# Argmax in its PSUM tile, logits turned ahead of the weighted sums, masks on other engines, late weights converted in the first batch

## The chip, the core and the metric

The kernel runs on one core of one Trainium2 chip. The metric is the device time in microseconds (us) of one execution, as a median over several. Four compute engines work side by side, each with a queue of its own that it runs in order: TensorE (PE; PEld is its loading of weights), VectorE (DVE), ScalarE (ACT) and GpSimd (POOL). SyncE (SP) issues nearly all transfers, also in order.

## The reference

The inputs q, k and v have 4 batches, 8 heads, 768 positions and 64 columns per head. In the first part each position attends only to positions of its own cluster; in the second the result x (768 x 512 per batch) is rotated by an angle, mixed over the positions, and passed through a channel product.

```python
q_assign = np.argmax(np.einsum('bhsd,hcd->bhsc', q_n, c_n), axis=-1)   # 16 clusters per head
k_assign = np.argmax(np.einsum('bhsd,hcd->bhsc', k_n, c_n), axis=-1)
mask = q_assign[:, :, :, None] == k_assign[:, :, None, :]
scores = np.where(mask, 0.125 * np.matmul(q, k.transpose(0, 1, 3, 2)), -1e9)
attn = np.exp(scores - np.max(scores, axis=-1, keepdims=True))
attn = attn / (np.sum(attn, axis=-1, keepdims=True) + 1e-09)
x = np.matmul(attn, v)                       # heads side by side: 4 x 768 x 512

theta = x @ w_theta
zr, zi = x * np.cos(theta), x * np.sin(theta)
y = np.einsum('ts,bsd->btd', w_tok_r, zr) + np.einsum('ts,bsd->btd', w_tok_i, zi)
u = x + y
out = u + np.maximum(u @ w_ch, 0.0)
```

q, k, v and the centroids are 32-bit floats. The four weight matrices are 64-bit floats; the kernel loads their raw words and makes 32-bit floats of them itself.

## The kernel before, in words

**Attention.** Two heads make a pair; there are 16 pairs (4 batches of 4). A pair is cut into 12 units (`NU`): 2 halves of the queries (a) times 6 blocks of 128 keys (i). The main loop takes two units per round, u and u + 1. In a round TensorE makes the scores of unit u, then the scores of unit u + 1 interleaved with products that give the row maximum of a unit ten units ahead (`ahead = u + LEAD`). Those products go to tiles "m" of the PSUM pool `ps0`, which has two of them in rotation. `max_of` on the vector engine reduces each to nm (L396). Between the two interleaved halves, j = 1 first and j = 0 second, stand the weighted sums av (L509) of the two units before.

Products are kept exact by splitting a number into a rounded part (hi) and the rest (lo): hq, lq, hk, lk for the pair, hi and lo for each weight. The mask is a product too: mq and mk (128 x 768) hold, at row c of each head, whether a position belongs to cluster c, scaled so that a pair of positions of different clusters gets a huge negative score. Row 32 carries the row maximum to be subtracted.

**Small steps of a pair** are generators whose pieces are filed under unit numbers (`at_unit`, `stages`). A round runs three batches of pieces: those up to u - 0.5 before the weighted sums, those up to u behind them, those up to u + 1 at the end of the round; within a batch in order of the number. `in_order` then chains the instructions of each engine in exactly this order, so in the attention no planner moves them. A planner with its own costs does place the instructions of the second part, and it may begin them while the attention still runs.

`assign(pi)` prepares pair pi two pairs ahead. Its pieces, with the numbers of `A_UNITS` counted from the start of pair pi - 2: load q and k (-9); multiply with the centroids (lg, L263) and copy (-4); turn the logits with three transposes on TensorE into the tile lt (L275), reduce to the maximum (L278) and mark where the logits equal it (eq, L280) (-2); multiply eq by a column of numbers that fall with c (L284) and reduce again, which gives the cluster number with ties to the first (L286) (-1); turn it (2), store it (2), load it back spread over 16 rows per head as clq and clk (3); make mq by an absolute value (L335, 6) and a cut-off at zero (L337, 7) on ScalarE, for pair 1 with one GpSimd instruction (L333); make mk on the vector engine (L339, 7.9). lt takes an "m" tile from pair 2 on. `A_SECOND` and `A_THIRD` are the numbers for pairs 1 and 2.

Other small steps on the same queues: `add_exps` sums the exponentials in threes on GpSimd (L448); `add_sums` adds two such sums on the vector engine (L452) at units 8 and 13 of the pair; `sums` reduces them over the keys, and its row goes through memory in four steps with numbers `SUMS`: store sd, load sq, take the reciprocal (L494) and store, load rb; `normalise` multiplies.

**Weights.** `early_weights` converts w_theta and the first three row blocks (t = 0, 1, 2) of both mixing matrices during the attention: load 768 KB of raw words (L130), an absolute value on ScalarE (L135), four operations on the vector engine (L137, L140, L143, L146), hi on ScalarE (L158), lo on GpSimd (L159). The row blocks t = 3, 4, 5 are converted there too, but kept in DRAM as 32-bit floats (L156, tiles wd3r to wd5i); one block starts every `W_EVERY` = 12 units, sixteen in all.

**Second part.** For each of 24 blocks (b, t) of 128 positions `theta` makes the angle (tp, L608, then kk and r on the vector engine, L613 to L615) and `rotate` the parts z; `mix` multiplies with the row block t of the weights into y (L876), and after t = 5 `channel(b)` makes the channel product (L899). In batch 0, `late` is advanced once per block before its `mix`: it loads a kept block, splits it (L790 on ScalarE, L791 on the vector engine), and from t = 5 on converts w_ch in four row blocks. Its buffers are the four tiles "u" (`u_tile`), which the channel stage then uses for itself. `first_rotation` begins the first block at the end of the attention.

## Time and profile before

| | us |
|---|---|
| median of 3 runs | 791.12 (791.0 to 792.93) |
| profiled execution | 792.87 |
| its span, first to last instruction | 791.1 |
| TensorE busy in the span | 774.3 (98%) |
| VectorE busy | 572.6 (72%) |
| GpSimd busy | 488.3 (62%) |
| ScalarE busy | 386.5 (49%) |
| mean granted TensorE clock | 0.991 of full speed |

The attention fills the span to about 452 us, the second part the rest. In 40 slices of the span (about 20 us each) the busy share, in tenths, reads so; the third row is GpSimd:

```
PE   6999999999999999999999799999999999999998
DVE  5789999999999999999989659954445433634322
POOL 3388789999999999888988432561215122332131
```

In the profile's rows, `out<-in` names the tile written and the tiles read, `[0.58 <-PE m L374]` behind a row says how long the engine sat idle before it and what ended that, and xN is a number of like instructions. TensorE's matmuls overlap, so the busy time of a group can be more than its share of the span.

### The profile page before, as it was taken

To read this page: it belongs to the slowest core of one execution; us is meant where nothing else is said; L and a number is where in the kernel's file an instruction comes from. 1 tells how busy PE (TensorE), PEld (TensorE's weight loads), DVE (VectorE), ACT (ScalarE), POOL (GpSimd) and SP (SyncE) were. 2 spreads that over 40 slices of the span, in tenths; PEclk is the share of its full clock that TensorE was granted. 3 is DMA by queue.
4 is the path that set the end of the run, shared out by engine and by line. 5 is a ranking of instruction groups with operands and counts; after the bars stand their busy time and mean duration, and the time that the engine had idled before them with its cause. 6 is when DMAs were issued, how large, how long until landed. Compare 5 with 4: busy or idle time off the path is not lost.

```text
span 791.1 us, 14306 instructions
## 1 busy us (share of the span) xinstructions
PE 774.3 (98%) x5538; PEld 572.9 (72%) x5538; DVE 572.6 (72%) x688; ACT 386.5 (49%) x777; POOL 488.3 (62%) x284
## 2 busy tenths in 40 slices
PE   6999999999999999999999799999999999999998
PEld 4656665666656565656665488899889988899998
DVE  5789999999999999999989659954445433634322
ACT  3366666767676676767556436341334123403310
POOL 3388789999999999888988432561215122332131
PEclk9899999999999999999999999999999999999999
DMA  3132324332433244324343467115011411030001
GB/s 120 61 98 72 93 95 151 93 123 91 151 104 125 81 149 151 119 84 164 112 161 109 101 182 206 24 31 173 15 27 28 160 27 27 14 94 15 1 21 61
DMA packets 81583, 73.43 MB, mean 93 GB/s; under 512 B 59588, under 2 KB 65324, under 8 KB 81132
## 3 DMA queue, kind: packets, MB, share of 16 engines
q1 hardware_dynamic: 81228, 72.10, 30.5%
q8 instruction: 43, 0.70, 0.4%
q10 hardware_dynamic: 288, 0.43, 0.1%
q14 instruction: 24, 0.20, 0.1%
HBM read 57.08 MB, written 15.32 MB: 92 GB/s over the span
## 4 chain that ended last, share of the span: by engine, by line
PE 91%; DVE 5%; DMA 2%; issue 1%; SPq 1%; ACT 1%; DVEq 0%
PE y L876 26%; PE sc L374 24%; PE av L509 15%; PE tp L608 8%; PE cy L899 5%; PE m L374 4%; PE cp L899 3%; PE sm L476 2%; PE lg L263 2%; PE y L899 1%; DVE acc L452 1%; PE lt L275 1%; DVE nm L396 1%; PE mt L404 1%; DVE xl L583 1%
## 5 line engine op out<-in xcount | busy, mean ns | idle before, releaser
L437 ACT ACTIVATE at<-sc 128x384 f32<-128x384 f32 x384 | 173.6, 493 | 96.0 <-PE m L374 50.5
L396 DVE TENSOR_REDUCE nm<-m 128x1 f32<-128x768 f32 x192 | 179.6, 945 | 21.4 <-PE m L374 18.3
L448 POOL TENSOR_TENSOR acc<-at,at 128x768 f32<-128x768 f32 x64 | 129.9, 2030 | 36.0 <-ACT at L437 36.0
L374 PE MATMUL m<-hk,hq 64*128 64x384 f32 x384 | 147.1, 387 | 0.9 <-DVE nm L396 0.8
L509 PE MATMUL av<-at,vt 128*64 128x384 f32 x768 | 145.7, 499 | 1.4 <-ACT at L437 1.2
L830 POOL TENSOR_TENSOR zlc<-ab,zhc 128x512 fp32r<-128x512 f32 x24 | 32.1, 1336 | 173.2 <-ACT zhc L828 173.2
L448 POOL TENSOR_TENSOR acc<-acc,at 128x768 f32<-128x768 f32 x64 | 132.4, 2068 | 10.1 <-ACT at L437 8.0
L374 PE MATMUL m<-mk,mq 64*128 64x384 f32 x384 | 127.7, 336 | 0.8 <-DVE mk L303 0.8
L374 PE MATMUL sc<-hq,hk 64*128 64x384 f32 x384 | 116.6, 388 | 0.5 <-ACT at L437 0.5
L374 PEld LDWEIGHTS sc<-hq,hk 64*128 64x128 f32 x384 | 55.8, 184 | 62.7 <-issue 27.9
L374 PE MATMUL sc<-mq,mk 64*128 64x384 f32 x384 | 97.6, 335 | 0.0
L374 PE MATMUL sc<-hq,lk 64*128 64x384 f32 x384 | 97.3, 334 | 0.0
L374 PE MATMUL sc<-lq,hk 64*128 64x384 f32 x384 | 97.3, 334 | 0.0
L509 PEld LDWEIGHTS av<-at,vt 128*64 128x64 f32 x768 | 46.7, 136 | 60.5 <-issue 53.6
L374 PEld LDWEIGHTS m<-hk,hq 64*128 64x128 f32 x384 | 70.7, 185 | 3.4 <-DVE nm L396 2.8
L374 PEld LDWEIGHTS m<-mk,mq 64*128 64x128 f32 x384 | 71.6, 188 | 1.1 <-ACT hq L356 1.1
L613 DVE TENSOR_SCALAR kk<-tp 128x512 int32<-128x512 f32 x24 | 16.4, 683 | 77.2 <-PE tp L608 77.2
L452 DVE TENSOR_TENSOR acc<-acc,acc 128x768 f32<-128x768 f32 x30 | 70.6, 2354 | 0.0
L581 ACT CAST xh<-xT 128x512 fp32r<-128x512 f32 x23 | 14.3, 622 | 99.7 <-PE tp L608 99.7
L890 POOL TENSOR_TENSOR ul<-xT,uh 128x384 fp32r<-128x384 f32 (+1 forms) x36 | 33.5, 957 | 35.4 <-ACT uh L889 34.9
L374 PEld LDWEIGHTS sc<-lq,hk 64*128 64x128 f32 x384 | 54.9, 186 | 0.0
L374 PEld LDWEIGHTS sc<-mq,mk 64*128 64x128 f32 x384 | 54.7, 184 | 0.0
(160 smaller groups left out, 1710.3 us busy)
## 6 DMA issues: line engine op xcount, KB each, us to landing
rawq<-in_qT_dram SPq DMA_DIRECT2D x16, 384.0 KB
vt<-in_v_dram SPq DMA_DIRECT2D x16, 384.0 KB
rb<-sd SPq DMA_DIRECT2D x32, 192.0 KB
xT_d<-xt SPq DMA_DIRECT2D x16, 384.0 KB
xb<-xT_d SPq DMA_DIRECT2D x96, 64.0 KB
rawk<-in_kT_dram SPq DMA_DIRECT2D x15, 384.0 KB
w<-in_wrT_dram SPq DMA_DIRECT2D x6, 768.0 KB
w<-in_wiT_dram SPq DMA_DIRECT2D x6, 768.0 KB
```

The costliest lines, as they stand in the source:

```text
L374: nc.tensor.matmul(out, lhsT=stat[r, cols], rhs=mov[r, over], start=start, stop=stop)
L396: nc.vector.tensor_reduce(out=s["nm", a][:, j, i // 2:i // 2 + 1], in_=s["m", j][:, :, 0:HS], op=ALU.max, axis=AX.XY, negate=True)
L437: last_exp[0] = nc.scalar.activation(out=s["at", a, i][:, j], in_=s["sc", j], func=AF.Exp, scale=SCALE)
L448: last_acc[0] = nc.gpsimd.tensor_tensor(out=s["acc", a, x], in0=prev, in1=at, op=ALU.add)
L452: nc.vector.tensor_tensor(out=s["acc", a, 0], in0=s["acc", a, 0], in1=s["acc", a, 1], op=ALU.add)
L509: nc.tensor.matmul(s["av"][64 * j:64 * j + 64], lhsT=s["vt"][:, i, j, :], rhs=s["at", a, i][:, j], start=(i == 0), stop=(i == NT - 1))
L608: nc.tensor.matmul(tp, lhsT=xx[:, c, :], rhs=w_th[c][k], start=(n == 0), stop=(n == 3 * NCT - 1))
L613: nc.vector.tensor_scalar_mul(kk, tp, INV_2PI)
L830: nc.gpsimd.tensor_tensor(out=zl, in0=tr, in1=zh.bitcast(F32), op=ALU.subtract)
L876: nc.tensor.matmul(y_at(b, d, c0, c1), lhsT=zz[:, d * P:(d + 1) * P], rhs=ww[:, c0:c1], start=first and lead, stop=last, skip_group_check= ...
L890: nc.gpsimd.tensor_tensor(out=ul[:, d, :], in0=x, in1=uh[:, d, :].bitcast(F32), op=ALU.subtract)
L899: nc.tensor.matmul(cp, lhsT=w_c[d][k][:, e * P:(e + 1) * P], rhs=uu[:, d, :], start=(n == 0), stop=(n == 3 * NCT - 1), skip_group_check=True)
```

## The change

- **Argmax.** The equality is written over the logits in their own PSUM tile, and the product with the falling numbers reads it from there and comes in the same piece, in front of the yield.
- **Order.** The piece that turns the logits moves from -2 to -2.5 (for pair 2 from 0 to -0.5), that is, from behind the weighted sums of its round to in front of them.
- **Masks.** mk is made on ScalarE by one absolute value with a scale and an offset per row (rows c: 2^60 times the distance of the cluster numbers; row 32: one). mq is made on the vector engine, -1 where the number is c. The ScalarE pieces at 6 and 7 become one at 7, and pair 1 is like the others. The scale and the offset are filled behind the first pair's preparation.
- **Late weights.** The row blocks t = 3, 4, 5 are no longer converted in the attention and kept; `late` converts them in the first batch from the raw words, in two chunks of 384 columns each, like w_ch. `LATE` says after which of the ten row blocks it yields: two blocks each before the products of t = 0 and 1, three before t = 2, two before t = 3, one before t = 4. The ten early ones start at other units (0, 12, 36, 48, 72 and so on).

```diff
+LATE = (1, 3, 6, 8)
...
-    ncl = cpool.tile([P, 1], F32, name="ncl")
-    nc.vector.tensor_scalar_mul(ncl, mcl, -1.0)
+    kscale = cpool.tile([P, 1], F32, name="kscale")
+    kbias = cpool.tile([P, 1], F32, name="kbias")
+    def mask_constants():
+        nc.vector.memset(kscale, 0.0)
+        nc.vector.memset(kbias, 0.0)
+        for r in (0, 64):
+            nc.vector.memset(kscale[r:r + C], BIG)
+            nc.vector.tensor_scalar_mul(kbias[r:r + C], mcl[r:r + C], -BIG)
+            nc.vector.memset(kbias[r + 32:r + 33], 1.0)
...
         nc.vector.tensor_tensor(
-            out=eq, in0=ltv, in1=mx.unsqueeze(2).broadcast_to([P, NG, C]), op=ALU.is_equal)
-        yield
-        nc.vector.tensor_tensor(out=eq, in0=eq, in1=wb, op=ALU.mult)
+            out=ltv, in0=ltv, in1=mx.unsqueeze(2).broadcast_to([P, NG, C]), op=ALU.is_equal)
+        nc.vector.tensor_tensor(out=eq, in0=ltv, in1=wb, op=ALU.mult)
+        yield
...
-        mq = st[pi]["mq"]
-        if pi == 1:
-            nc.gpsimd.tensor_scalar(out=mq, in0=cl["q"], scalar1=mcl, scalar2=None, op0=ALU.is_equal)
-        else:
-            nc.scalar.activation(out=mq, in_=cl["q"], func=AF.Abs, bias=ncl)
-            yield
-            nc.scalar.activation(out=mq, in_=mq, func=AF.Relu, scale=-1.0, bias=1.0)
+        nc.scalar.activation(out=st[pi]["mk"], in_=cl["k"], func=AF.Abs, scale=kscale, bias=kbias)
         yield
         nc.vector.tensor_scalar(
-            out=st[pi]["mk"], in0=cl["k"], scalar1=mcl, scalar2=mbi, op0=ALU.not_equal, op1=ALU.mult)
+            out=st[pi]["mq"], in0=cl["q"], scalar1=mcl, scalar2=-1.0, op0=ALU.is_equal, op1=ALU.mult)
...
-        for t in range(EARLY, NT):
-            for x, src in (("r", wrT), ("i", wiT)):
-                yield from split_w(
-                    None, None, src[t * P:(t + 1) * P], S, raw_pair, nc.gpsimd, CKE, kept=w_d[t, x])
...
-    A_UNITS = (-9, -4, -2, -1, 2, 2, 3, 6, 7, 7.9)
+    A_UNITS = (-9, -4, -2.5, -1, 2, 2, 3, 7, 7.9)
...
-    A_THIRD = (-9, -1, 0, 1, 4, 4, 5, 7, 8, 9)
-    W_EVERY = 12
+    A_THIRD = (-9, -1, -0.5, 1, 4, 4, 5, 8, 9)
...
     part_lo(0, "k", nc.gpsimd)
+    mask_constants()
...
-        stages(W_FIRST if x == 0 else [W_EVERY * (x - 1) + k for k in W_UNITS], gen)
+        stages(W_FIRST if x == 0 else [NU * (3 * (x - 1) // 2) + k for k in W_UNITS], gen)
...
     def late():
-        for t in range(EARLY, NT):
-            for w, x in ((w_r, "r"), (w_i, "i")):
-                hi, lo = w[t]
-                kept = u_tile("kept").rearrange("p c s -> p (c s)").bitcast(F32)[:, 0:S]
-                nc.sync.dma_start(out=kept, in_=w_d[t, x])
-                nc.scalar.copy(out=hi, in_=kept)
-                nc.vector.tensor_tensor(out=lo, in0=kept, in1=f(hi), op=ALU.subtract)
-            if t < NT - 1:
+        rows = [(w[t], src, S, t) for t in range(EARLY, NT) for w, src in ((w_r, wrT), (w_i, wiT))]
+        rows += [(w_c[c], w_ch, DM, c) for c in range(NCT)]
+        for x, (hi_lo_, src, cols, r) in enumerate(rows):
+            for gen in split_w(*hi_lo_, src[r * P:(r + 1) * P], cols, wt_pair, nc.gpsimd, CK):
+                run(gen)
+            if x in LATE:
                 yield
-        for c in range(NCT):
-            if c:
-                yield
-            for gen in split_w(*w_c[c], w_ch[c * P:(c + 1) * P], DM, wt_pair, nc.gpsimd, CK):
-                run(gen)
```

More of the change, by code (lines that the diff above doesn't have):

```diff
@@ L148, in to_f32, with split_w @@
         return w
-    def split_w(hi, lo, src, cols, new, eng, most, kept=None):
+    def split_w(hi, lo, src, cols, new, eng, most):
         def chunk(sl):
@@ L154, in chunk @@
             yield
-            if kept is not None:
-                nc.sync.dma_start(out=kept[:, sl], in_=w)
-                return
             nc.scalar.copy(out=hi[:, sl], in_=w)
@@ L173 @@
     w_c = {}
-    w_d = {(t, x): dram.tile([P, S], F32, name=f"wd{t}{x}") for t in range(EARLY, NT) for x in "ri"}
     ma = [ctx.enter_context(tc.tile_pool(name="ma0", bufs=1))]
```

## The prediction

> **What bounds the kernel now.** I read the page's chain of work that ended last first, then that chain in order of time.
>
> ```profile
> PE 91%; DVE 5%; DMA 2%; issue 1%; SPq 1%; ACT 1%; DVEq 0%
> 95.34 1.03 PE sc L374 x10
> 121.83 1.03 PE sc L374 x10
> 148.31 1.03 PE sc L374 x10
> 174.26 1.03 PE sc L374 x10
> ```
>
> TensorE holds 91% of the chain. The four rows are the same matmuls in consecutive pairs of heads. A settled pair takes 174.26 - 148.31 = 25.95 us; the two before it take 26.49 and 26.48. So the attention runs at TensorE's pace, and two pairs lose 0.53 us each. The change gives TensorE no matmul less: what counts is whether TensorE waits more or less often. Every wait comes from the vector queue, so I read that queue around the place where the logits are turned (lt, L275), beside the GpSimd queue, in the timeline of one settled pair.
>
> ```profile
> 179.77 0.96 DVE L396 TENSOR_REDUCE nm<-m 128x1 f32<-128x768 f32 x1 [0.58 <-PE m L374]
> 180.65 1.22 DVE L339 TENSOR_SCALAR mk<-clk,mcl,mbi 128x768 fp32r<-128x768 f32 x1
> 181.79 2.59 DVE L452 TENSOR_TENSOR acc<-acc,acc 128x768 f32<-128x768 f32 x1
> 184.31 0.94 DVE L396 TENSOR_REDUCE nm<-m 128x1 f32<-128x768 f32 x1
> ...
> 179.64 1.81 POOL L448 TENSOR_TENSOR acc<-acc,at 128x768 f32<-128x768 f32 x1
> 181.41 2.15 POOL L448 TENSOR_TENSOR acc<-at,at 128x768 f32<-128x768 f32 x1
> ...
> 184.51 1.51 PE L509 MATMUL av<-at,vt 128*64 128x384 f32 x8
> 185.96 0.55 PE L275 MATMUL lt<-identf,lgs 128*128 128x128 f32 x3
> ```
>
> The columns are start and duration in us. The reader is to see an order that the program fixes: a row maximum (nm), the mask mk, the sum of the exponentials acc, the next nm. The first nm waits 0.58 us for TensorE, so the vector engine has no backlog there. Then mask and sum take 3.8 us, though neither is slow by itself:
>
> ```profile
> 30.82 0.67 DVE L339 TENSOR_SCALAR mk<-clk,mcl,mbi 128x768 fp32r<-128x768 f32 x1
> 412.81 0.95 DVE L452 TENSOR_TENSOR acc<-acc,acc 128x768 f32<-128x768 f32 x1
> ...
> 35.64 1.83 POOL L448 TENSOR_TENSOR acc<-at,at 128x768 f32<-128x768 f32 x1 [5.72 <-ACT at L437]
> ```
>
> The difference is GpSimd, which at 30.82 had been idle (its row: 5.72 us before 35.64). In the settled pair the mask ends 0.42 us after the GpSimd addition that began at 179.64 ended (181.45); the sum ends 0.82 us after the next addition ended (183.56). Each is thus held for the rest of a GpSimd instruction, about 1.8 us when whole.
>
> **The turned logits: the main term.** Today L275 stands behind the weighted sums (L509). TensorE begins these at 184.51 and the transposes at 185.96, without waiting. The transposes write the second of the two "m" tiles, whose last reader is the nm of 184.31, which ends at 185.25. Before the change the weighted sums cover that nm: 1.45 us of matmuls stand between. The change puts unit -2.5 in place of -2, so the transposes come in the half round before the weighted sums, where TensorE is ready at 184.51. They then wait until about 185.29: 0.75 us. Behind them on TensorE's queue stand the weighted sums and all later scores, so the wait is lost in full; no later stall is there to absorb it, since the chain of a settled pair is TensorE alone. The order on the vector queue in front (nm, a mask at 7.9, the sum at 8, nm) is kept by the change; only the mask is now mq instead of mk, the same 128x768 operation from cluster numbers to two-op result. I cost it as mk. TensorE changes its kind of matmul as often in the new order as in the old, so the order itself costs nothing.
>
> How often: for pairs 4 to 15, twelve times. Pair 2 is turned before any weighted sum exists; in front of pair 3 the sum comes at unit 7, before the nm, so I give it nothing. In two early pairs the queue is later than in the settled ones:
>
> ```profile
> 79.48 1.51 PE L509 MATMUL av<-at,vt 128*64 128x384 f32 x8
> 79.79 0.94 DVE L396 TENSOR_REDUCE nm<-m 128x1 f32<-128x768 f32 x1
> ...
> 105.61 1.51 PE L509 MATMUL av<-at,vt 128*64 128x384 f32 x8
> 107.29 0.55 PE lt L275 x3
> ```
>
> For pair 4 the nm ends at 80.73 and TensorE is ready at 79.48: 1.3 us. For pair 5 it is 107.29 - 105.61 = 1.7 us. Pair 6 looks like pair 5 before (a 512-column weight chunk being converted) but has no chunk after the change: 0.75. Pair 7 then gets that chunk: between 0.75 and 1.7, I take 1.2. Eight settled ones at 0.75 make 6.0. Sum 1.3 + 1.7 + 0.75 + 1.2 + 6.0 = 10.95 us. The two losses of 0.53 are inside these waits, so 1.06 goes off: +9.9 us. The bounds depend on how much of a GpSimd instruction is left when the mask comes: with none left the mask and the sum take about 0.45 + 1.83 + 0.83 = 3.1 us and the wait is 0.15 us (twelve: 1.8 - 1.06 = +0.7); with a whole one it is near 1.8 us (12 x 1.83 - 1.06 = +20.9). I take the middle value, since unit 7's addition on GpSimd ends near 181.4 with or without the weight conversions.
>
> **Argmax's equality and product.** The equality writes the logits' own tile, and the product reads it there, in front of the next yield.
>
> ```profile
> L284 DVE TENSOR_TENSOR eq<-eq,wc 128x384 bf16<-128x384 bf16 x16 | 22.2, 1387 | 0.1
> L280 DVE TENSOR_TENSOR eq<-lt,mxl 128x384 bf16<-128x384 f32 x16 | 8.9, 557 | 0.6
> ```
>
> ```profile
> 12.14 0.37 DVE eq L284
> ```
>
> The product takes 1387 ns on average now, since it too waits for GpSimd, and 0.37 us where GpSimd is idle. Reading the PSUM tile I cost it like L280, 557 ns, which is never held. So the vector queue gains 0.83 us a pair in the steady part. This buys nothing: after the turn the nm waits for TensorE anyway. At the start, for pairs 0 and 1, the chain passes through these rows, and 0.2 us is added twice: +0.4 us. The product also passes one nm on the vector queue; that nm comes behind the weighted sums on TensorE, 1.45 us later, so it is not delayed. The tile is held 0.56 us longer; its next writer comes two rounds of matmuls later (over 2 us), so this is covered, and if it were not, 0.5 us a pair would be added.
>
> The Trainium skill's page VectorE: DVE Perf Modes (section "Why PSUM operands drop a tier") speaks against this edit: a product of 16-bit SBUF tensors may run at double rate, an fp32 PSUM operand brings it down to single rate. By it alone the product would be slower everywhere, an estimate of 0.2 us for each of 16. Its page SBUF — State Buffer (section "Who interferes with whom") says the opposite of the sum: an instruction with one SBUF input does not contend with GpSimd, one with two does. The rows 1387 and 557 ns side with the second; the sum is the same by either, because the product is off the chain but for the start.
>
> **Masks.** One ScalarE activation per pair is dropped and the other moves to mk; ScalarE is not on the settled chain. The first pair's mask leaves GpSimd, which is idle there. The few column-wide constants follow the first mk, at 15.96, where the vector engine idles until the next nm. Nothing for all of it.
>
> **Late weights, attention side.** Six conversions (four vector operations, a load, a store) leave. In the settled part they cost TensorE nothing, so nothing comes back. At the end they do:
>
> ```profile
> 436.87 0.32 SPq L156 DMA_DIRECT2D wd5i<-w  x1
> 437.47 1.07 PE L608 MATMUL tp<-wth_hi,xl 128*128 128x512 f32 x4
> 439.37 0.23 DVE L494 RECIPROCAL sq<-sq 128x12 f32<-128x12 f32 x1 [2.53 <-DMA sq<-sd]
> 441.01 1.16 PE L608 MATMUL tp<-wth_hi,xh 128*128 128x512 f32 x4 [1.40 <-DVE r L614]
> ```
>
> The store wd5i waits for its conversion and holds the SP queue; behind it the load of sq comes late, the reciprocal waits 2.53 us for it, and behind that stands the chain to r (L614), for which TensorE waits 1.40 us. Without the store the next to be late is the product tp itself: kk can start when tp ends, at 438.5 by its last row, instead of behind the reciprocal that ends at 439.6: -1.1 us.
>
> **Late weights, first batch.** Each 128x768 weight block now comes as two 384-column chunks of raw 64-bit data through four buffers, is converted, copied and split; GpSimd does the subtraction that L791 did.
>
> ```profile
> 455.00:471.00 16.00, 16.00 (x80) 13.03 (x74) 8.27 (x14) 7.14 (x12) 6.38 (x5) 0.89 0.54 146
> 471.00:482.00 11.00, 11.00 (x61) 9.45 (x60) 7.71 (x11) 5.03 (x8) 0.00 (x0) 1.00 0.65 196
> 482.00:493.00 11.00, 11.00 (x61) 9.44 (x61) 10.93 (x15) 6.50 (x11) 3.58 (x2) 1.00 0.93 282
> 493.00:504.00 11.00, 11.00 (x61) 9.48 (x60) 11.00 (x16) 4.05 (x8) 6.06 (x5) 1.00 0.16 26
> 504.00:516.00 12.00, 12.00 (x66) 10.32 (x65) 9.10 (x12) 6.02 (x11) 5.91 (x4) 1.00 0.14 22
> 516.00:527.00 11.00, 11.00 (x65) 9.97 (x64) 9.55 (x21) 8.08 (x16) 8.11 (x7) 1.00 0.23 37
> ...
> L137 DVE TENSOR_SCALAR wtmp<-wtmp 128x512 f32<-128x512 f32 x4 | 2.8, 693 | 0.0
> L140 DVE TENSOR_SCALAR wtmp<-wtmp 128x512 int32<-128x512 int32 x4 | 2.1, 536 | 0.0
> L143 DVE SCALAR_TENSOR_TENSOR wtmp<-wtmp 128x512 int32<-128x512 int32 x4 | 3.8, 958 | 0.0
> L146 DVE SCALAR_TENSOR_TENSOR wtmp<-wtmp 128x512 int32<-128x512 int32 x4 | 2.7, 680 | 0.0
> L791 DVE TENSOR_TENSOR wr_lo<-kept,wr_hi 128x768 fp32r<-128x768 f32 x3 | 4.0, 1318 | 0.1
> 493.38 8.41 PE y L876 x48
> ```
>
> The windows' third pair of numbers is the vector engine's busy time: 56.6 of 72 us, so 15.4 us are free before the channel stage. A chunk costs (693 + 536 + 958 + 680) x 384/512 = 2150 ns; twelve cost 25.8 us, less the six subtractions (4.0 us for wr, as much for wi) 17.9 us. That is 2.5 us more than is free, and the row block of t = 3 is wanted at 493.38, the others 11.2 us apart. I take +2.5 us. At the least it is 0 (chunks packed between, theta's work of the next batch put off to the channel stage); if the 7.7 us free before 471 cannot be used because the raw data has not landed, 17.9 - 7.7 = 10.2.
>
> **The sum.** +9.9 + 0.4 - 1.1 + 2.5 = +11.7 us. The profiled execution took 792.87 us (span 791.1 and 1.8 around it) and would take 804.6; the median of the runs is 791.12, 1.75 lower: 802.8 us.
>
> **Rivals.** (1) The vector queue's relief reaches further: mask and sum together stay under 2.8 us, because GpSimd, freed from the conversions, is idle when the mask comes (their rows without it: 0.67 + 0.95). Then the nm ends before 184.5, the transposes never wait, the two early losses vanish (-1.06), and the end of the attention gives back half of what TensorE idles there (15.00 - 10.38 us in the window below): -1.06 + 0.4 - 1.1 - 2.3 = -4.1, 787.0 us.
>
> ```profile
> 440.00:455.00 15.00, 10.38 (x59) 5.21 (x59) 10.21 (x13) 7.06 (x13) 5.36 (x3) 0.88 0.47 109
> ```
>
> For it: less vector and GpSimd work. Against it: GpSimd runs without a gap from 179.64 to past 183, and unit 7's addition cannot start before its exponentials. (2) The first batch becomes vector-bound by 10.2: 810.5 us; for it speaks 10.9 and 11.0 busy of 11 us in two windows, against it the idle stage behind. (3) The mask meets a GpSimd instruction at its beginning in every pair: +20.9 in place of 9.9, 813.8 us. (4) It meets one at its end: +0.7 + 0.4 - 1.1, the first batch hidden: 791.1 us, a change that does nothing.
>
> **How the numbers follow.** Forecast 0.46, (1) 0.13, (2) 0.21, (3) 0.07, (4) 0.13. Range 787.5 to 813: it holds the forecast, (2), (4) and the upper half of (1). A measurement tells a change from none at about 0.3%, 2.4 us. Faster: 0.12, most of (1). Within: 0.14, (4) and the weak edge of (1). Slower: 0.74.
>
> **What would show it.** Right: TensorE gaps of 0.5 to 1.1 us in front of L275 in pairs 4 to 15, ended by nm, and a period near 26.7 us; the product near 0.56 us and unheld; no SP store before the sq load; vector windows full from 471 to 527. Wrong: a period of 25.95 us with lt ahead of the weighted sums, or a stall of several microseconds in front of t = 3, 4, 5 or the channel product.

## The result and the profile after

The changed kernel takes 819.1 us (median of four runs, 816.95 to 819.88), the kernel before 792.02 us beside it (four runs, 791.0 to 793.49): a ratio of 1.0336, 95% interval 1.0308 to 1.0364. The forecast was 802.8 us with a range of 787.5 to 813.0: the sign was right, the time lies above the range.

The page of the changed kernel first: the shares of the chain of work that ended last.

```profile
PE 72%; DVE 13%; DMA 8%; issue 3%; ACT 2%; SPq 0%; POOL 0%; DVEq 0%; ACTq 0%
```

TensorE held 91% of that chain before and holds 72% now; the vector engine has gone from 5% to 13%, the transfers from 2% to 8%. To see where, I cut both traces at three instructions: the load of the sine table, which follows the last exponential of the attention on ScalarE; the first channel product of the first batch (cp); and the first angle product (tp) behind it. First the kernel before, then the changed one, from the timelines. Of both also the first of the sums x + y (`add_y`), which the channel product reads; of the kernel before also the reciprocal of the last row sums, the last store of xT_d and the first cast of a late weight; of the changed kernel also a wait inside the token products (y).

```profile
449.52 1.28 ACT L823 ACT_TABLE_LOAD   x1
464.64 0.18 DVE L494 RECIPROCAL sq<-sq 128x12 f32<-128x12 f32 x1
472.44 0.33 SPq L533 DMA_DIRECT2D xT_d<-xt  x1
478.85 0.84 ACT L790 CAST wr_hi<-kept 128x768 fp32r<-128x768 f32 x1
519.04 0.74 DVE L887 TENSOR_TENSOR xT<-y,xT 128x384 f32<-128x384 f32 x2
523.93 0.51 PE L899 MATMUL cp<-uh,wch_hi 128*128 128x384 f32 x2
540.59 1.08 PE L608 MATMUL tp<-wth_hi,xh 128*128 128x512 f32 x4
```

```profile
457.20 1.28 ACT L811 ACT_TABLE_LOAD   x1
525.64 0.62 PE L864 MATMUL y<-wi_hi,zhs 128*128 128x512 f32 x2 [1.45 <-ACT wi_hi L164]
543.90 0.74 DVE L875 TENSOR_TENSOR xT<-y,xT 128x384 f32<-128x384 f32 x2
545.10 1.01 PE L887 MATMUL cp<-uh,wch_hi 128*128 128x384 f32 x2 [10.79 <-ACT uh L877]
566.56 1.08 PE L603 MATMUL tp<-wth_hi,xh 128*128 128x512 f32 x4
```

The attention ends 7.68 us later. From there to the channel product it takes 87.90 us instead of 74.41 (+13.49), and the channel product takes 21.46 instead of 16.66 (+4.80). Together 25.97 us; the span has grown by 26.1, so the rest of the kernel is unchanged. The +13.49 are TensorE's waits, 13.6 us in sum: 10.79 us in front of the channel product and 2.8 us for late weights inside the token products (the row of 525.64 and two shorter ones), where the kernel before has none. The forecast for the attention was +9.2 (9.9 + 0.4 - 1.1), for the first batch +2.5: the first is near, the second is short by 15.8 us.

**The attention.** Three pairs of the changed kernel, on TensorE the transposes that write lt (the wait in front of them stands in brackets), and the vector queue ahead of them.

```profile
101.98 2.07 DVE L338 TENSOR_SCALAR mq<-clq,mcl 128x768 fp32r<-128x768 f32 x1
107.49 0.55 PE L280 MATMUL lt<-identf,lgs 128*128 128x128 f32 x3 [1.58 <-DVE nm L395]
...
129.59 0.84 DVE L338 TENSOR_SCALAR mq<-clq,mcl 128x768 fp32r<-128x768 f32 x1
133.86 0.55 PE L280 MATMUL lt<-identf,lgs 128*128 128x128 f32 x3 [0.34 <-DVE nm L395]
...
183.62 1.20 DVE L338 TENSOR_SCALAR mq<-clq,mcl 128x768 fp32r<-128x768 f32 x1
184.74 2.58 DVE L451 TENSOR_TENSOR acc<-acc,acc 128x768 f32<-128x768 f32 x1
187.25 0.94 DVE L395 TENSOR_REDUCE nm<-m 128x1 f32<-128x768 f32 x1
188.25 0.55 PE L280 MATMUL lt<-identf,lgs 128*128 128x128 f32 x3 [0.69 <-DVE nm L395]
```

The waits are there, ended by the row maximum nm, with mask, sum and maximum in front of it as forecast. Their size follows the mask: 0.34 us where it takes 0.84 us, 0.69 where it takes 1.20, 1.58 where it takes 2.07. These are pairs with no weight chunk, with a 768-column chunk and with a 512-column one, in this order. In pair 4, the first of the twelve, the mask takes 0.61 us and there is no wait. In sum (us, number of waits, the longest):

```profile
PE lt L280 <- DVE nm L395: 8.0, 11, 1.6
```

The product, from the groups by line:

```profile
L287 DVE TENSOR_TENSOR eq<-lt,wc 128x384 bf16<-128x384 f32 x16 | 8.9, 558 | 0.5
```

The product takes 558 ns (1387 before, 557 forecast) and is never held. The end of the attention went as forecast too: TensorE waits 0.52 us for r where it waited 1.40.

```profile
448.70 1.15 PE L603 MATMUL tp<-wth_hi,xh 128*128 128x512 f32 x4 [0.52 <-DVE r L609]
```

**The first batch.** The windows of the changed kernel (length, then busy time with the number of instructions for PE, its weight loads, DVE, ACT and POOL, then granted clock, DMA share and GB/s):

```profile
471.00:482.00 11.00, 11.00 (x64) 9.58 (x63) 10.07 (x20) 3.10 (x5) 2.76 (x2) 1.00 0.28 58
482.00:493.00 11.00, 11.00 (x61) 9.45 (x60) 4.96 (x8) 4.68 (x9) 3.09 (x4) 1.00 0.69 207
493.00:504.00 11.00, 11.00 (x61) 9.47 (x60) 8.50 (x14) 5.82 (x12) 6.36 (x6) 1.00 0.67 169
504.00:516.00 12.00, 11.49 (x62) 9.63 (x61) 11.96 (x20) 3.65 (x8) 5.65 (x5) 1.00 0.58 145
516.00:527.00 11.00, 8.80 (x45) 7.02 (x43) 10.99 (x16) 6.83 (x13) 7.29 (x6) 1.00 0.40 118
527.00:538.00 11.00, 7.22 (x40) 6.10 (x40) 11.00 (x18) 5.60 (x10) 5.02 (x4) 0.92 0.39 108
538.00:549.00 11.00, 3.54 (x7) 1.90 (x8) 11.00 (x18) 4.70 (x9) 6.82 (x7) 0.50 0.15 24
```

The third pair is the vector engine. It idles for 8.5 us between 482 and 504 (6.04 + 2.50), and is then full until 549. What the buffers wait for, in order of time:

```profile
474.77 0.18 DVE L493 RECIPROCAL sq<-sq 128x12 f32<-128x12 f32 x1
484.17 0.33 SPq L532 DMA_DIRECT2D xT_d<-xt  x1
490.82 0.93 ACT L164 CAST wr_hi<-wtmp 128x384 fp32r<-128x384 f32 x2 [1.97 <-DMA xT_d<-xt]
493.43 0.62 SPq L139 DMA_DIRECT2D wtmp<-in_wrT_dram  x1
```

Four chunks are loaded and converted by 478, and fill the four buffers. The cast of the first (wr_hi) waits until the last pair's normalised rows (xT_d) have landed, 6.6 us after that store was issued, and only when GpSimd has subtracted are buffers free and the next chunk's load is issued (493.43). The store itself is 4.1 us later than before, counted from the end of the attention (27.0 us instead of 22.9). Of this, 2.5 us come from the reciprocal of the last row sums, which stands behind conversions on the vector queue: 17.6 us after the end of the attention (474.77 - 457.20) instead of 15.1 (464.64 - 449.52). In the kernel before the same cast also follows the same store by 6.4 us, but there all later vector work on these weights is six subtractions, and no token product waits.

### The profile page after: what moved, and what is told of

Read it like the earlier page. It is cut to its first block, busy times and chain, and to the rows that moved or that the text cites. A ratio compares the mean times of both kernels' runs of the same rounds, so it can differ in the third digit from the quotient of the medians.

```text
span 817.2 us, 14363 instructions
## 1 busy us (share of the span) xinstructions
PE 778.9 (95%) x5538; PEld 575.1 (70%) x5538; DVE 549.2 (67%) x713; ACT 379.6 (46%) x776; POOL 486.6 (60%) x295
## 4 chain that ended last, share of the span: by engine, by line
PE 72%; DVE 13%; DMA 8%; issue 3%; ACT 2%; SPq 0%; POOL 0%; DVEq 0%; ACTq 0%
PE sc L373 19%; PE y L864 19%; PE av L508 13%; PE tp L603 6%; PE cy L887 5%; PE m L373 3%; DVE acc L451 3%; PE cp L887 3%; DMA vt<-in_v_dram 2%; DMA sd<-se 2%; DVE nm L395 2%; DVE mq L338 2%; PE sm L475 1%; DVE wtmp L152 1%; PE y L887 1%
## 5 line engine op out<-in xcount | busy, mean ns | idle before, releaser
L447 POOL TENSOR_TENSOR acc<-at,at 128x768 f32<-128x768 f32 x64 | 124.4, 1943 | 57.9 <-ACT at L436 57.9
L447 POOL TENSOR_TENSOR acc<-acc,at 128x768 f32<-128x768 f32 x64 | 127.6, 1994 | 19.4 <-ACT at L436 17.5
L878 POOL TENSOR_TENSOR ul<-xT,uh 128x384 fp32r<-128x384 f32 (+1 forms) x36 | 34.3, 980 | 34.3 <-ACT uh L877 33.7
```

Of the source, the lines that this page charges most:

```text
L447: last_acc[0] = nc.gpsimd.tensor_tensor(out=s["acc", a, x], in0=prev, in1=at, op=ALU.add)
L878: nc.gpsimd.tensor_tensor(out=ul[:, d, :], in0=x, in1=uh[:, d, :].bitcast(F32), op=ALU.subtract)
```

## The experiments

All ratios are to the kernel before, run beside on the same chip; intervals are 95%. The kernel before had medians of 790.9 to 791.8 us beside the runs, 792.02 beside the changed kernel. "Attention" is the time of the sine table's load in the profiled run, "to cp" and "cp to tp" the two stretches behind it, in us.

| run | median | ratio | attention | to cp | cp to tp |
|---|---|---|---|---|---|
| before | 792.02 | 1 | 449.52 | 74.41 | 16.66 |
| changed | 819.1 | 1.0336 (1.0308 to 1.0364) | 457.20 | 87.90 | 21.46 |
| a_lt2 | 814.09 | 1.0285 (1.0260 to 1.0309) | 452.84 | 86.07 | 20.74 |
| a_kept | 804.28 | 1.0171 (1.0135 to 1.0208) | 464.99 | 74.38 | 16.66 |
| b_lt25 | 803.18 | 1.0147 (1.0120 to 1.0173) | 460.19 | 74.39 | 16.66 |
| b_late | 809.46 | 1.0233 (1.0206 to 1.0260) | 448.25 | 87.48 | 21.04 |
| a_lt2_kept | 797.79 | 1.0067 (1.0041 to 1.0093) | 454.37 | 73.44 | 16.67 |
| a_lt2_sb | 809.61 | 1.0206 (1.0170 to 1.0242) | 449.74 | 87.09 | 21.84 |
| a_sb | 819.92 | 1.0360 (1.0323 to 1.0397) | 462.72 | 87.41 | 21.86 |
| a_split | 814.52 | 1.0275 (1.0244 to 1.0307) | 457.69 | 83.21 | 20.61 |
| a_twice | 821.83 | 1.0378 (1.0331 to 1.0426) | 458.52 | 87.24 | 22.92 |
| a_split_wch | 815.52 | 1.0300 (1.0271 to 1.0330) | 464.06 | 78.47 | 18.97 |
| a_split_wch_v | 813.33 | 1.0287 (1.0247 to 1.0327) | 465.57 | 76.03 | 20.54 |
| a_keep | 820.63 | 1.0383 (1.0359 to 1.0408) | 458.65 | 86.63 | 22.86 |
| a_all | 800.72 | 1.0119 (1.0100 to 1.0139) | 451.20 | 77.38 | 18.98 |
| b_w | 790.80 | 0.9992 (0.9981 to 1.0002) | 448.82 | 73.44 | 16.66 |

### Which part costs what

**a_lt2**: the changed kernel, the transposes behind the weighted sums again.

```diff
-    A_UNITS = (-9, -4, -2.5, -1, 2, 2, 3, 7, 7.9)
+    A_UNITS = (-9, -4, -2, -1, 2, 2, 3, 7, 7.9)
-    A_THIRD = (-9, -1, -0.5, 1, 4, 4, 5, 8, 9)
+    A_THIRD = (-9, -1, 0, 1, 4, 4, 5, 8, 9)
```

> The changed kernel with the logits turned behind the weighted sums again (unit -2, for the third pair unit 0); all else as changed. Theory 1, two separate losses: the place of the turned logits makes the attention's 7.7 us and nothing else, the first batch's 18.3 us stay. Then no gap in front of the transposes lasts over 0.2 us, a settled pair takes 25.95 to 26.1 us, and the time is 819.1 - 8 = 811 us (808 to 813). Rival: the vector queue is as late in either order, and TensorE waits behind the weighted sums instead: 817 to 819 us.

814.09 us, just above the range of theory 1 and below that of the rival. The waits in front of lt are gone, yet a settled pair takes 26.30 us, not 25.95. The loss has moved into the matmuls behind the transposes. TensorE and the vector queue of a_lt2, then TensorE of the kernel before at the same place:

```profile
292.19 0.55 PE L280 MATMUL lt<-identf,lgs 128*128 128x128 f32 x3
293.97 0.56 DVE L287 TENSOR_TENSOR eq<-lt,wc 128x384 bf16<-128x384 f32 x1
294.20 0.43 PE L373 MATMUL sc<-hq,hk 64*128 64x384 f32 x1
294.67 0.41 PE L373 MATMUL m<-hk,hq 64*128 64x384 f32 x1
```

```profile
291.80 0.44 PE L374 MATMUL sc<-hq,hk 64*128 64x384 f32 x1
291.90 0.41 PE L374 MATMUL m<-hk,hq 64*128 64x384 f32 x1
```

The maximum product m comes 0.47 us after the score product beside it, instead of 0.10. It writes the tile of the turned logits, which the product (293.97 + 0.56 = 294.53) still reads. So theory 2: in this order the product costs 0.35 us a pair. Two runs test it from both sides.

**a_lt2_sb**: a_lt2 with equality and product as in the kernel before; masks and late weights stay changed.

```diff
         nc.vector.tensor_tensor(
-            out=ltv, in0=ltv, in1=mx.unsqueeze(2).broadcast_to([P, NG, C]), op=ALU.is_equal)
-        nc.vector.tensor_tensor(out=eq, in0=ltv, in1=wb, op=ALU.mult)
+            out=eq, in0=ltv, in1=mx.unsqueeze(2).broadcast_to([P, NG, C]), op=ALU.is_equal)
         yield
+        nc.vector.tensor_tensor(out=eq, in0=eq, in1=wb, op=ALU.mult)
```

> The changed kernel with the logits turned behind the weighted sums, and the equality again in SBUF with the product half a unit later, as before; the new masks and the late weights stay. Theory 2: the 0.35 us per pair go, a settled pair takes 25.95 us, 809 to 811 us. Rival, the masks make it (mq by the vector engine in place of mk): a pair stays at 26.3 us, 813 to 815 us.

**a_lt2_kept**: a_lt2 with the late weights kept in DRAM as in the kernel before.

```diff
-        stages(W_FIRST if x == 0 else [NU * (3 * (x - 1) // 2) + k for k in W_UNITS], gen)
+        stages(W_FIRST if x == 0 else [12 * (x - 1) + k for k in W_UNITS], gen)
...
+        for t in range(EARLY, NT):
+            for x, src in (("r", wrT), ("i", wiT)):
+                yield from split_w(
+                    None, None, src[t * P:(t + 1) * P], S, raw_pair, nc.gpsimd, CKE, kept=w_d[t, x])
...
-        rows = [(w[t], src, S, t) for t in range(EARLY, NT) for w, src in ((w_r, wrT), (w_i, wiT))]
+        for t in range(EARLY, NT):
+            for w, x in ((w_r, "r"), (w_i, "i")):
...
+                nc.sync.dma_start(out=kept, in_=w_d[t, x])
+                nc.scalar.copy(out=hi, in_=kept)
+                nc.vector.tensor_tensor(out=lo, in0=kept, in1=f(hi), op=ALU.subtract)
```

> The changed kernel with the turned logits behind the weighted sums again and the late weights kept in DRAM as before: of the change the equality in PSUM with its product and the masks are left. Theory 2: the product holds the second m tile 0.56 us longer on the vector engine, and the next maximum product that writes it waits 0.35 us in each of 13 pairs: a settled pair of 26.3 us, 795 to 797 us. Rival, the prediction's step (covered by two rounds of matmuls): 791 to 793 us.

809.61 us, settled pairs of 25.95 to 26.01 us, and 797.79 us, settled pairs of 26.29 to 26.34: theory 2 holds, and the masks, which a_lt2_sb keeps, cost the settled pair next to nothing.

**a_sb**: the changed kernel with equality and product as before, the transposes left in front of the weighted sums.

> The changed kernel with equality and product as before (equality into SBUF, product half a unit later), the transposes still in front of the weighted sums. Theory 2b: the 0.35 us of the product are lost only where the transposes stand behind the weighted sums; in front of them 1.45 us of matmuls lie between and cover it: pairs of 26.3 and 26.7 us as in the changed kernel, 817 to 820 us. Rival, it costs in either order: 813 to 815 us.

819.92 us, no difference from the changed kernel (its profiled run ends the attention later because it lost 2.4 us ahead of the second pair): in front of the weighted sums the product costs nothing. The two losses do not add; the wait in front of lt takes the place of the one behind it. In one pair of this run the mask met a whole GpSimd instruction:

```profile
186.75 2.23 DVE L338 TENSOR_SCALAR mq<-clq,mcl 128x768 fp32r<-128x768 f32 x1
192.40 0.55 PE L280 MATMUL lt<-identf,lgs 128*128 128x128 f32 x3 [2.39 <-DVE nm L395]
```

The mask takes 2.23 us and TensorE waits 2.39, more than the 1.83 that rival 3 set for every pair. The profiled runs of a_kept, a_split_wch and a_split_wch_v have such a pair too (2.38 to 2.40 us).

**b_lt25**: the kernel before with -2.5 and -0.5 as the transposes' units, nothing else.

> The kernel before with one thing changed: the logits are turned at unit -2.5, in front of the weighted sums (-0.5 for the third pair). Theory 1: 12 or 13 waits of 0.7 to 1.6 us, ended by the row maximum, 8 to 12 us, 800 to 804 us. Rival: the mask and the sum behind a GpSimd instruction are what decides, and with the old masks the maximum comes in time: 791 to 794 us.

803.18 us; the attention ends 10.67 us later. The view of waits:

```profile
PE lt L275 <- DVE nm L396: 11.4, 12, 1.7
```

Twelve waits, 11.4 us, with 0.73 to 0.77 in the settled pairs, where every pair has a chunk.

**b_late**: the kernel before with the late weights of the change alone (the edit of a_lt2_kept the other way round).

> The kernel before with the late weights of the change alone: no conversion of t = 3 to 5 during the attention, they come with w_ch in the first batch in the new order. Theory 1: the first batch loses 18 us, the attention gains 1 to 2 us at its end: 808 to 811 us. Rival, the prediction's own step: the vector engine's free time takes in nearly all of it, and what was lost in the changed kernel came with the later end of the attention: 793 to 798 us.

809.46 us. The attention ends 1.27 us earlier, the stretch behind it takes 17.45 us longer (13.07 + 4.38). So this loss needs no later end of the attention.

**a_kept**: the changed kernel with the late weights kept in DRAM (the edit of a_lt2_kept).

> The changed kernel with the late weights of before: t = 3 to 5 converted during the attention, kept in DRAM, loaded and split in the first batch; a chunk in every pair again. Theory 1: the 18.3 us of the first batch go, the waits for the turned logits stay and grow to about 0.7 us in each pair, since each has a chunk again: 801 to 804 us. Rival: the stall in the first batch comes from the later end of the attention and of its last stores, not from the conversions: 812 us or more.

804.28 us, and the two stretches are back at 74.38 and 16.66. (Its profiled run lost 2.6 us ahead of the second pair and waited 2.4 us for one mask, so its end of the attention is not compared.)

### Why the first batch loses 18 us

Two theories were stated: R, the buffers are held until the last store of the attention has landed; V, the vector engine has no time left.

**a_split**: the pool of the late weights cut in three.

```diff
-    m1 = mctx.enter_context(tc.tile_pool(name="m1", bufs=1))
+    m1 = {t: mctx.enter_context(tc.tile_pool(name=f"m1{t}", bufs=1)) for t in range(EARLY, NT)}
...
-        w_r[t] = hi_lo(m1, f"wr{t}", S)
-        w_i[t] = hi_lo(m1, f"wi{t}", S)
+        w_r[t] = hi_lo(m1[t], f"wr{t}", S)
+        w_i[t] = hi_lo(m1[t], f"wi{t}", S)
```

> The changed kernel with the pool of the late weights cut into one pool for each row block, at the same addresses. The halves of t = 3 then lie on no memory that the last pair's normalised rows or sums held, so their first cast needs no longer the landing of the last xT_d store (490.8 us in the changed kernel). Theory R, late release: the first four buffers come free at about 479 to 481 us, the next loads start some 11 us earlier, the vector engine works in the stretch 482 to 504 where it had 8.5 us free, and the wait in front of the channel product falls from 10.8 us to 2 to 5: 810 to 813 us. Theory V, vector capacity alone: the vector engine is full later in any case and nothing but the order of its work changes: 817 to 820 us.

```profile
471.92 0.51 ACT L164 CAST wr_hi<-wtmp 128x384 fp32r<-128x384 f32 x1 [2.22 <-DVE wtmp L155]
482.00:493.00 11.00, 11.00 (x61) 9.47 (x60) 8.49 (x12) 2.52 (x6) 5.84 (x4) 1.00 0.92 300
493.00:504.00 11.00, 11.00 (x61) 9.44 (x61) 10.90 (x18) 6.20 (x13) 6.75 (x6) 1.00 0.43 99
540.90 1.01 PE L887 MATMUL cp<-uh,wch_hi 128*128 128x384 f32 x2 [4.36 <-ACT uh L877]
```

The first cast comes 18.9 us earlier, the vector engine idles 2.6 us between 482 and 504 instead of 8.5, the wait in front of cp falls from 10.79 to 4.36. 814.52 us: the two stretches give back 5.5 us of 18.3 (109.36 to 103.82). R is shown for this part. The edit leaves size and order of these tiles alone, so by the program they lie at the same addresses (no run shows addresses). That the cast waited all the same points to the rule by which the memory is handed over: a new pool waits for all that the old pools under it held, here the last pair's rows, also where the tile itself lies elsewhere. The vector engine is then full from 493 to 538, and 12.8 us remain.

**a_twice**: more vector work in the same place.

```diff
         nc.vector.tensor_scalar(
             out=w, in0=w, scalar1=F64_LEAST, scalar2=F64_MOST, op0=ALU.max, op1=ALU.min)
+        if new is not raw_pair:
+            nc.vector.tensor_scalar(
+                out=w, in0=w, scalar1=F64_LEAST, scalar2=F64_MOST, op0=ALU.max, op1=ALU.min)
```

> The changed kernel with the clamp of each late chunk done twice on the vector engine (the second changes no value): 12 more instructions of 0.54 us and 4 of 0.89 us, 10.0 us of vector work. Theory V, and any theory in which the vector engine sets the end of the first batch once the buffers move: all but the first four chunks' 2.1 us come back in the wait for the channel product, +6 to +9 us, 825 to 828 us. Rival, the loads and GpSimd's subtractions between two uses of a buffer set the pace: +0 to +2 us, 819 to 821 us.

821.83 us, 2.7 us above the changed kernel with overlapping intervals; in the trace the two stretches are 0.8 us longer (110.16 against 109.36). V by itself would have it at 825 or more. The timeline of the vector queue says why:

```profile
544.57 0.74 DVE L878 TENSOR_TENSOR xT<-y,xT 128x384 f32<-128x384 f32 x2
545.23 0.68 DVE L155 SCALAR_TENSOR_TENSOR wtmp<-wtmp 128x512 int32<-128x512 int32 x1
```

The sum of y (add_y, L878 here) begins at 544.57, 0.7 us later than in the changed kernel, and conversions of w_ch now follow it. Some of the added work also went into the vector engine's gaps before 504 (6.7 us idle between 482 and 504 instead of 8.5). So the amount of vector work does not set the end of the stage by itself. The planner changed the order along with the amount, so this run does not isolate the order; that what stands in front of add_y sets the end is so far inferred.

**a_split_wch**: a_split, and w_ch, whose four blocks stood in front of add_y, converted in the attention (so that every pair has a chunk again).

```diff
+        for c in range(NCT):
+            yield from split_w(None, None, w_ch[c * P:(c + 1) * P], DM, raw_pair, nc.gpsimd, CKE, kept=w_d[c])
...
+            if src is w_ch:
+                nc.sync.dma_start(out=kept, in_=w_d[r])
+                nc.scalar.copy(out=hi_lo_[0], in_=kept)
+                nc.gpsimd.tensor_tensor(out=hi_lo_[1], in0=kept, in1=f(hi_lo_[0]), op=ALU.subtract)
```

> The changed kernel with the pool of the late weights cut in three, and w_ch converted during the attention, kept in DRAM and only loaded, cast and subtracted in the first batch; t = 3 to 5 stay late. This takes 4 x 3.3 = 13.2 us of vector work out of the stage. If vector time is what is left of the loss once the buffers are released early, the first batch's loss (12.6 us with the pool cut alone) falls to 0 to 3 us, while the attention has a chunk in every pair again (+1 to 3 us): 803 to 807 us. Rival, the rest of the loss is where add_y stands among the rotations of the next tokens, or the landing of the loads: 811 to 815 us.

815.52 us: no gain in the time, but not for the rival's reason. The two stretches fall by 6.4 us, from 103.82 to 97.44, and cp starts without a wait; the attention gives the same amount away, since each pair with a 512-column chunk now waits 1.6 us in front of lt, the last three too, and one pair 2.4. My expectation had put +1 to 3 us there and should have taken 1.6 from the rows above. Of what is left, 6.4 us, the view of TensorE's waits shows 4.6: 3.0 us in the token products (2.1 for zlc on GpSimd, 0.9 for zhc on ScalarE) and 1.6 in the channel product for uh. One of the waits ahead of lt, and the longest of the token products:

```profile
353.06 0.55 PE L284 MATMUL lt<-identf,lgs 128*128 128x128 f32 x3 [1.60 <-DVE nm L399]
533.21 0.89 PE L876 MATMUL y<-wr_hi,zlc 128*128 128x512 f32 x2 [2.12 <-POOL zlc L830]
```

**a_split_wch_v**: the same with the late subtractions on the vector engine.

```diff
-                nc.gpsimd.tensor_tensor(out=hi_lo_[1], in0=kept, in1=f(hi_lo_[0]), op=ALU.subtract)
+                nc.vector.tensor_tensor(out=hi_lo_[1], in0=kept, in1=f(hi_lo_[0]), op=ALU.subtract)
...
-                for gen in split_w(*hi_lo_, src[r * P:(r + 1) * P], cols, wt_pair, nc.gpsimd, CK):
+                for gen in split_w(*hi_lo_, src[r * P:(r + 1) * P], cols, wt_pair, nc.vector, CK):
```

> The kernel with the pool cut and w_ch kept, with the late subtractions on the vector engine instead of GpSimd. Theory G: part of what is left of the first batch's loss (6.4 us) comes from GpSimd, whose subtractions stand in front of the rotation's low halves (a wait of 2.1 us for zlc) and hold the vector engine's two-input operations (a late 384-column chunk takes 2.54 us, its parts unheld 1.8 us); then 3 to 5 us come back: 810 to 813 us. Theory V: vector time is what is short, and 12 subtractions of some 0.6 us and 4 of 0.7 us on it cost more than GpSimd's absence gives: 816 to 821 us.

813.33 us, between the two and not to be told from the run before. The wait for zlc is gone, another of 1.21 us for wi_lo has come, and the two stretches are 0.9 us shorter (96.57). The chunk's parts do get shorter, to 443 + 434 + 639 + 636 = 2.15 us by their groups, from 2.54; the subtraction (545 ns unheld) uses that up. How the last 6.4 us divide between the vector engine and GpSimd stays open.

**a_keep**: the changed kernel with TensorE kept busy through its wait, to see what makes the channel product slower.

```diff
+KEEP = 56
...
     def channel(b):
+        if b == 0:
+            with tc.issue_after(last_y[0].ins):
+                for _ in range(KEEP):
+                    nc.tensor.matmul(
+                        ys[0][5][:, 128:512], lhsT=zero, rhs=w_r[0][0][:, 0:HS],
+                        start=False, stop=True, skip_group_check=True)
```

> The changed kernel with 56 matmuls put between the last token product of the first batch and the channel product; they add zeros to a finished y bank, need nothing that is late, and fill about 10 us of TensorE's 10.8 us wait. Theory C: the channel product takes 21.5 us instead of 16.7 because TensorE stood still before it and was granted a clock of 0.50 and 0.67 for the first 10 us; kept busy it takes 16.7 to 17.5 us, and the time falls by 4 to 5 us: 814 to 816 us. Rival, the clock is set by something else, or the filling delays the adds: 818 us or more.

```profile
534.48 9.87 PE L904 MATMUL y<-wr_hi,zero 128*128 128x384 f32 x56
545.28 0.44 PE L891 MATMUL cp<-uh,wch_hi 128*128 128x384 f32 x1 [0.92 <-ACT uh L881]
548.97 2.47 PE L891 MATMUL cp<-uh,wch_hi 128*128 128x384 f32 x5 [3.26 <-ACT uh L881]
545.00:547.00 2.00, 0.44 (x1) 0.19 (x1) 2.00 (x5) 0.99 (x3) 1.97 (x2) 0.99 0.00 0
547.00:549.00 2.00, 0.03 (x1) 0.03 (x1) 2.00 (x5) 2.00 (x5) 1.00 (x2) 0.50 0.00 0
```

```profile
547.00:549.00 2.00, 1.86 (x4) 0.79 (x4) 2.00 (x5) 2.00 (x5) 1.19 (x2) 0.50 0.00 0
```

The first fence is a_keep (matmuls, then two windows), the second the changed kernel's window at the same place; the number behind the five busy times is the granted clock. The filling did hold the clock at 1.00 up to 545, and bought nothing: 820.63 us, and cp to tp takes 22.86 us. At full clock the product runs into the next wait after one matmul (3.26 us for uh), since add_y has only begun, and in that wait the clock falls to 0.50 again. In the changed kernel the clock is 0.50 at this point and the same matmuls are simply slow. Theory C fell as the main cause: the channel product is fed by add_y, which stands behind the conversions. The last piece of add_y ends 6.31 us after the first channel product in the changed kernel (551.41) and 1.85 us after it in the kernel before (525.78); from there to tp it takes 15.15 and 14.81 us. In a_all below, add_y ends 4.95 us after the first channel product, the clock is 1.00 throughout, and tp follows 14.03 us later. By this comparison the low clock has about 1 of the 4.8 us, an estimate; no run isolates it.

### Is there a version that beats both?

**a_all**: a_split_wch with the transposes, equality and product as in the kernel before (the edits above together).

> As the run before, and the logits turned behind the weighted sums with equality and product as in the kernel before. If the three causes found (the place of the transposes, the product in the vector queue, the late conversions) are all of the loss, the time is that of before: 790 to 794 us. If something of the change is not named yet: 796 us or more.

800.72 us, so something of the change is not covered by the causes found. The attention has come to within 1.7 us of before, the two stretches keep 5.3 us (77.38 + 18.98 against 91.07): the six row blocks of t = 3 to 5, converted late, still cost that much with both causes taken away.

**b_w**: the kernel before with the last kept chunk 1.5 units earlier.

```diff
-        stages(W_FIRST if x == 0 else [W_EVERY * (x - 1) + k for k in W_UNITS], gen)
+        stages(W_FIRST if x == 0 else [min(W_EVERY * (x - 1), 12 * 14 - 1.5) + k for k in W_UNITS], gen)
```

> The kernel before with the last kept chunk converted 1.5 units earlier, so that its store no longer stands in front of the load of sq. By the prediction's term for the end of the attention: the reciprocal's 2.53 us wait and half or more of TensorE's 1.40 us in front of tp go, -1.1 us, 789 to 791 us. Rival, the chunk then delays a maximum or a load of the last pairs: 792 us or more.

790.80 us, ratio 0.9992 (0.9981 to 1.0002): as forecast in size, and not to be told from the kernel before. TensorE's wait in front of tp has fallen from 1.40 to 0.52 us:

```profile
440.30 1.16 PE L608 MATMUL tp<-wth_hi,xh 128*128 128x512 f32 x4 [0.52 <-DVE r L614]
```

No version tried beats the kernel before by more than the measurement is uncertain.

## Why the prediction was right or wrong

**What bounds the kernel: right.** In the attention nearly all of the loss is TensorE's wait for the vector queue.

**The turned logits, +9.9: mechanism right, size a little high.** The waits are in front of L280, ended by nm, in 11 of the 12 pairs named, 8.0 us in sum. b_lt25 shows that the rows of before were read rightly for the old vector queue: 0.73 to 0.77 us in the settled pairs against 0.75, 1.26 and 1.68 early against 1.3 and 1.7, 10.67 us in all. In the changed kernel every third pair has no chunk, and there the mask takes 0.84 us and the wait is 0.34 instead of 0.75. This is half of rival 1: the relief reaches the mask, but only in pair 4 (put at 1.3) far enough to end the wait. The order itself, put at nothing, is not quite free: less its wait, a settled pair takes 26.0 us in b_lt25 and 26.02 to 26.06 in the changed kernel, instead of 25.95. What makes this up to 0.1 us a pair stays open.

**Equality and product, 0 in the settled part: right in the kernel that was timed, wrong as a reason.** The price, 557 ns unheld, was right (558 ns). This agrees with the Trainium skill's page SBUF — State Buffer (section "Who interferes with whom"), by which an instruction with one SBUF input outside the two-port modes does not contend with GpSimd. The prediction gave that rule without its condition; it is no rule for every instruction with one SBUF input, for the mask reads one tensor from SBUF (and a column of scalars) and took from 0.61 to 2.23 us. I also wrote that the tile's next writer comes over 2 us later and so is covered. In the order of the kernel before it is not: a_lt2 loses 0.35 us a pair to it, as the alternative in the prediction had it (0.5). It is hidden in the changed kernel only because the transposes come earlier there.

**Start, end, masks.** The start: +0.13 us against +0.4 (the first weighted sums begin at 36.70 us instead of 36.57). The end of the attention: 0.88 us against 1.1. The masks: no cost seen in the settled pair. The attention as a whole: +7.68 against +9.2.

**Late weights, first batch, +2.5 with bounds 0 and 10.2: wrong; this step failed.** Measured +18.3. It compared a sum of vector work with a sum of free vector time, and three things in it did not hold. First the price: I scaled the 512-column rows to 2150 ns; the 384-column operations take 535 + 574 + 778 + 652 = 2539 ns, 4.7 us more in twelve chunks. Second the free time: of 15.4 us I let up to 7.7 be unusable, for raw data not landed. The first four chunks had landed and were converted by 478; they held the buffers, so the next load could not be issued before 493.43, and 8.5 us in the very middle of the stage (482 to 504) went by unused. a_split shows 5.5 us of the loss there. The release of memory was not among my waits at all, though the kernel before shows the store at the same place, where it holds up nothing. Third, a sum does not see the order: conversions of w_ch and add_y share a queue, and add_y, which before began at 519.0 while the token products were still running, begins at 543.9, 9.6 us after the last of them (534.3). Taking w_ch out gives back 6.4 us, adding 10 us of vector work costs 0.8 in the trace; that it is the order and not the amount is inferred from these two, no run changes the order alone. The channel product, which I had not costed, is 4.8 us slower, mostly because it follows add_y step by step. Of the rest, 6.4 us with both causes away, the division is not settled.

**Rival 2** (vector-bound first batch, 810.5) had the place right and the mechanism partly; its price stopped at 10.2. Rival 3 was seen in single pairs, rivals 1 and 4 did not come. Of the signs named beforehand, the gaps in front of L280 (0.34 to 1.60 us) spread wider than the 0.5 to 1.1 named, the vector windows full from 471 to 527 failed (4.96 of 11 us between 482 and 493), and the one named against the forecast, a stall of several microseconds in front of the channel product, came.

## What to carry to other kernels

When work is moved into a stage with idle engine time, don't compare sums: walk through the stage with its buffers, and ask what each first use of new memory waits for and which step of the stage's critical path will stand behind the moved work on an in-order queue. In a kernel that has one engine at its pace, a half round earlier for a step is only free when the engine that releases its tile is done by then; the rows of the old order say by how much it is late. And measure parts alone: the two attention edits here cost 6 us and 11 us alone (797.79 and 803.18) and 12 together (804.28), since one wait hides the other.

## What the runs showed of the hardware that was not expected

The granted clock of TensorE fell to 0.50 inside a wait, and not only in the 10.8 us one: 1.9 us after the end of the last token product in the changed kernel (534.3 to 536.2), and 1.2 us after the end of the channel product's first matmul in a_keep (545.7 to 547.0). It was back at 1.00 at 553.3 and 553.8: some 4.8 us after the matmuls had begun to follow one another in a_keep (548.97), some 8.2 us after the first of them in the changed kernel (545.10). Read from windows of 0.25 us, the changes of the clock lie whole multiples of 3.41 us apart: 461.15, 464.56, 536.24 and 553.31 in the changed kernel (1, 21 and 5 times), 546.96 and 553.78 in a_keep (2 times). The Trainium skill's page TensorE: Matmul & The Clock Gate (section "What's actually happening") gives half rate after an idle window of about 3.4 us and full rate after one busy window of that length. The trace agrees on the half and on the length. It differs in that the window before a fall was not idle throughout (the one up to 536.24 still held 1.5 us of matmuls), and in that the changed kernel took longer than one window to rise, with its first matmuls still interrupted.

One and the same 128x768 mask took 0.61 us at its shortest, and 0.84, 1.20, 2.07 or (in a_sb) 2.23 us while GpSimd additions of 1.8 to 2.2 us ran beside it; TensorE's wait grew with it, from 0.34 to 2.39 us.
